# Linear attention, gated convolution and gMLP in one kernel: products of zeros on an idle TensorE, a corrected transfer model and new keys

## The chip, the cores and the metric

The kernel runs on one core of a Trainium2 chip. The metric is the device time of one launch in microseconds, the median of three runs. The core's engines are TensorE (PE, with its weight loads PEld), VectorE (DVE), ScalarE (ACT), GpSimd (POOL) and the SyncE queue (SP), which issues all transfers here.

## The reference

Three stages follow each other, with batch 8, sequence 576, and float32 inputs (weights arrive as 64-bit floats):

1. Attention with a feature map, for 8 heads of 64 columns: `phi(x) = [exp(p), exp(-p)]` with `p = x w_phi - max|x w_phi|`, 128 features. Then `kv = phi(k)^T v`, `z = sum phi(k)`, and the output is `phi(q) kv / (phi(q) z + 1e-6)`.
2. A gated convolution over 512 channels: `sigmoid(conv5(x)) * (x w_val)`, times `w_out`.
3. A gMLP: `h = relu(x w_in)` is cut into `u` and `v`, `v` is normalised over its 512 columns, mixed over the sequence by `w_spatial` (576 x 576) plus a bias, multiplied by `u`, and put through `moe2_w_out`.

## The kernel before, in words

**Tiling.** The heads go in pairs: 4 pairs in each of 8 batches, 32 pairs in all. A pair loads k, v and q with the head dimension on the partitions, projects them by `w_phi` (`project`), takes the maxima and exponentials (`kexp`, `qmax`, `qexp`), sums k's side against v (`kvacc`, `kvout`) and forms numerators and denominators (`num`) that `divide` brings together; the result is a tile of x. When the four pairs of a batch are done, `mlp` does the batch's convolution, the products with w_val, the second half (`vchunk`) and the first half (`uhalf`) of w_in, the spatial mixing (`spatial`) and the output (`outrows`). w_out and w_in are multiplied together once, at the start: `weights` forms 8 tiles `wg` and `wu` from four tiles of w_out and four of each half of w_in, so that stage 2's last product and stage 3's first are one. Large products are made three times with high and low parts (`three`); the attention's are in float32, each of which the trace shows as two matmul instructions.

**Weights.** `load_f64` brings a tile of 64-bit floats and rebuilds float32 from it by one ScalarE and four VectorE instructions. There are 20 such tiles and one small one for the convolution. All of this runs beside the attention of the first pairs. From pair 4 on (`WHOLE`) the last 64 rows of a pair are loaded on their own; from pair 5 on (`EARLY`) VectorE and ScalarE weigh the denominators ahead of TensorE.

**Memory.** Two arenas in SBUF (`fa` float32, `ra` rounded float32) and the 8 banks of PSUM (`pa`) are handed out by `Arena.take` and `Arena.give`, which for the first 150 us of the plan's time prefers places that have rested.

**The order.** Nothing is issued while the kernel is described: each operation goes into a `Plan` with the engines that could do it, a modelled duration and a key. `Plan.order` (L234) then simulates the five engines: at each event every free engine takes, among its ready operations, the one with the least key, if buffers are free, and if the key is no more than `WINDOW` over the oldest key not yet started. A key's unit is one batch. The constants at the top of the file (L33 to L43) place the keys of each kind of operation: `AK_...` and `AQ_...` for a pair's k and q sides (eighths of a batch), `W_...` for the weights, `M_...` for the mixing layers. `READY` is when each engine begins in the model, `Clock` a model of TensorE's clock, and `FA_HOLD` and `RA_HOLD` room that operations ahead of their time leave free. Transfers are modelled by one number, the time at which the last one has gone through. `Plan.emit` (L341) issues the operations in the order found; every engine then runs its own in that order, and waits for data by semaphores.

**Lines in the profile.** The helpers issue everything, so L396 is any ScalarE or VectorE instruction, L431 POOL, L441 a transfer, L452 the three-part products (`gemm`), L465 all other products (`products`).

The two lines that place the first pair's loads before (L758, L763):

```
plan.key = (t + sub) / 8 * A_RATE - A_LEAD
at(t, AK_LOAD)
```

Of the kernel before, what the change touches and what calls it, by code (L numbers as in the profile page):

```python
# [10 lines left out]
F32 = mybir.dt.float32  # L11
# [8 lines left out]
B, H, S, D = 8, 8, 576, 64  # L20
F = 128
# [4 lines left out]
REM = 512  # L26
# [1 line left out]
DZ = D + 1  # L28
HALF = S // 2
TSPLIT = ((0, 256), (256, 320))  # L30
COLS = 28896
FA_COLS = 18176
A_LEAD, A_RATE = 1.4787, 1.0  # L33
AK_LOAD, AK_PROJ, AK_ACC, AK_SUM, AK_TURN = -0.2236, -0.128, -0.555, 0.2361, 2.6811
AQ_LOAD, AQ_MAX, AQ_EXP, AQ_NUM, AQ_HEAD, A_DIV = -0.4346, -0.0325, 0.8218, 3.0598, -0.0974, 5.3953
W_VAL, W_CONV, W_OUT, W_G, W_U, W_SP, W_OUT2, W_STEP = -1.6328, -1.2064, -0.8762, -0.9691, -0.5711, 0.3701, 0.0606, 0.072
M_CONV, M_VAL, M_V, M_U, M_SP, M_OUT, M_ALL = -0.3169, -0.2374, -0.148, 0.1029, -0.3397, 0.1352, 57.899
LONG_W, LONG_A, LONG_M = False, False, True
WINDOW = 0.4378
FA_HOLD = 3522  # L40
RA_HOLD = 4422
PA_HOLD = 0
LATER = 0.3845  # L43

MODE = 0.2419

EARLY = 5

WHOLE = 4

REST, SOON = 6.0, 150.0
READY = {"PE": 0.0, "ACT": 2.0, "DVE": 0.9, "POOL": 1.1, "SP": 0.6}
SIGNAL = {"PE": 0.2, "ACT": 0.145, "DVE": 0.13, "POOL": 0.2, "SP": 0.06}


# [2 lines left out]
SWITCH = 0.1  # L58

HELD = 1.0  # L60


class View:
# [29 lines left out]
class Buf(View):  # L93


    def __init__(self, model, cols, arena=None):
        super().__init__(self)
        self.model, self.cols, self.arena = model, cols, arena
        self.place = None if arena else model
        self.at = None  # L100
        self.base, self.writes, self.reads = [], [], []
        self.left, self.until = 0, 0.0
        self.long = False

    def note(self, op, reads, writes):
        deps = list(self.base)
# [94 lines left out]
class Plan:  # L201
# [5 lines left out]
        self.ops = []  # L207
        self.key = 0.0

    def add(self, ways, reads, writes, modes=(FULL, FULL), dma=False):  # L210

        op = Op()
        op.ways = ways
        op.n = len(self.ops)
        op.key = self.key
        op.modes, op.dma = modes, dma
        op.users, op.ready, op.start, op.end, op.way = [], 0.0, None, None, None
        seen = {}
        for group, w in ((reads, 0), (writes, 1)):
            for v in group:  # L220
                r = seen.setdefault(id(v.buf), [v.buf, False, False])
                r[1 + w] = True
        op.bufs = [r[0] for r in seen.values()]
        deps = {}
        for b, r, w in seen.values():
            for d in b.note(op, r, w):
                if d is not op:
                    deps[id(d)] = d
        op.need = len(deps)
        for d in deps.values():  # L230
            d.users.append(op)
        self.ops.append(op)

    def order(self, window, hold):  # L234

        ops = self.ops
        waiting = {e: [] for e in self.ENGINES}
        free = dict(READY)
        events = [0.0] + list(free.values())
        heapq.heapify(events)  # L240
        transfers, clock, mode = 0.0, Clock(), FULL
        frees = []
        by_key = sorted((o for o in ops if "POOL" not in o.ways), key=lambda o: (o.key, o.n))
        oldest = 0
        done = []
# [30 lines left out]
        while len(done) < len(ops):  # L276
# [13 lines left out]
            while again:  # L290
# [4 lines left out]
                for e in self.ENGINES:  # L295
# [6 lines left out]
                    for op in ready:  # L302
# [4 lines left out]
                        if e == "PE":  # L307
# [3 lines left out]
                            op.end = now + clock.run(now, busy, until)  # L311
                            busy = op.end - now
                        if op.dma:
                            transfers = max(transfers, now + busy + 0.63) + until
                            op.end = transfers + 0.85
                        free[e] = now + busy
                        if e == "POOL" and busy > 1.0:
                            free["DVE"] = max(free["DVE"], now) + HELD
# [17 lines left out]
                        again = True  # L336
                        forced = False
                        break
        return done

    def emit(self, window, hold):  # L341
        for op in self.order(window, hold):
            for b in op.bufs:
                if b.place is None:
                    b.place = b.arena.model(b.at[0] * b.arena.step, b.cols)
            op.ways[op.way][2]()
# [3 lines left out]
def attn_moe_gmlp_kernel(  # L350
# [19 lines left out]
    ctx.enter_context(tc.manual_schedule())  # L370

    plan = Plan()
    fa_t = const.tile([128, FA_COLS], F32, name="fa")
    ra_t = const.tile([128, COLS - FA_COLS], F32R, name="ra")
    banks = [ps.tile([128, 512], F32, name=f"bank{i}") for i in range(8)]
    fa = Arena(lambda o, n: fa_t[:, o:o + n], FA_COLS, 16)
    ra = Arena(lambda o, n: ra_t[:, o:o + n], COLS - FA_COLS, 16)
    pa = Arena(lambda o, n: banks[o // 512][:, 0:n], 8 * 512, 512)

    def fixed(shape, dtype, name):  # L380

        t = const.tile([shape[0], -(-shape[1] // 32) * 32], dtype, name=name)
        return Buf(t[:, 0:shape[1]], shape[1])
# [5 lines left out]
    def views(*xs):  # L389
        return [x for x in xs if isinstance(x, View)]  # L390
# [41 lines left out]

        plan.add({"POOL": (t, t, run)}, ins, [dest])

    def dma(out, in_, engine="SP"):
        n = 1
        for d in (out.shape() if isinstance(out, View) else out.shape):
            n *= d

        def run():  # L440
            (nc.sync if engine == "SP" else nc.scalar).dma_start(out=real(out), in_=real(in_))  # L441

        rows = (out.shape() if isinstance(out, View) else out.shape)[0]
        plan.add({engine: (0.475 if rows == 128 else 0.65, 4 * n / 385e3, run)}, views(in_), views(out), dma=True)

    def gemm(acc, terms, first=True, last=True):
        n = len(terms)
# [34 lines left out]


    warm = fixed([128, 8], F32, "warm")
    wphi = fixed([128, F], F32, "wphi")
    k4 = [fixed([128, F], F32, f"k4_{i}") for i in range(3)]
    q4 = [fixed([128, F], F32, f"q4_{i}") for i in range(3)]
# [4 lines left out]
    wr1 = fixed([128, S], F32R, "wr1")  # L492
    convw = fixed([128, 5 * KD], F32, "convw")
    rden = [Buf(dr.tile([2, S], F32, name=f"rden{i}"), S) for i in range(4)]

    def wtiles(name, n, width):
        return [[fixed([128, width], F32R, f"{name}{i}_{k}") for k in range(n)] for i in range(2)]
# [28 lines left out]
    def weights():  # L526
        def at(x):
            plan.key = x

        at(-2.0)  # L530
        dma(wphi, w_phi.unsqueeze(0).to_broadcast([2, D, F]))

        def fill(x, value):
            pool(0.1 + cols_of(x) / 960, "memset", x, [], x, value)


        fill(ones, 1.0)
        fill(warm, 0.0)
# [62 lines left out]
    def load_k(P):  # L601
        b, hp = divmod(P, NP)
        kl, vl = k4[P % 3], v4[P % 3]
        n = S if P < WHOLE else REM
        k, v = fa.buf(n), fa.buf(4 * 2 * VW)
        dma(k, kT[b, hp, :, 0:n])
        dma(v.rearrange("p (c d) -> p c d", c=4), v1[b, 0:REM, hp].rearrange("(c p) d -> p c d", p=128))

        if P < WHOLE:
            vt = fa.buf(2 * VW)  # L610
            dma(vt, v1[b, REM:S, hp].unsqueeze(0).to_broadcast([2, 64, 2 * VW]))
        for hh in range(2):
            r, d, o = half(hh), vcols(hh), slice(DZ * hh, DZ * hh + DZ)
            if P < WHOLE:
                copy(kl[r, r], k[r, REM:S])
                copy(vl[r, o], vt[r, d])
            else:
                dma(kl[r, r], kT[b, hp, r, REM:S])
                dma(vl[r, o], v1[b, REM:S, hp, d])
        return k, v, kl, vl  # L620
# [134 lines left out]
    def attention():  # L755
        n = B * NP

        def at(t, sub=0.0):  # L758
            plan.key = (t + sub) / 8 * A_RATE - A_LEAD

        for P in range(n):
            t = 2 * P
            at(t, AK_LOAD)  # L763
            k, v, kl, vl = load_k(P)
            at(t, AQ_LOAD)
            q, ql = load_q(P)
            at(t, AK_PROJ)
            kas, qas = project(k, kl, q, ql)
            at(t, AK_ACC)
            kp = [kexp(a, 4) for a in kas[0:2]]  # L770
# [237 lines left out]
```

## Time and profile before

| | |
|---|---|
| median of 3 runs | 853.55 us (851.74 to 854.84) |
| profiled execution | 857.97 us, of which span 856.2 us |
| TensorE busy | 824.4 us, 96% of the span, 7800 instructions |
| VectorE busy | 653.9 us, 76% |
| ScalarE busy | 495.9 us, 58% |
| GpSimd busy | 148.7 us, 17% |
| mean granted TensorE clock | 0.992 |
| transfers | 62.29 MB, mean 73 GB/s |

Times in the trace count from the first instruction of the span. A line of the timeline has the start, the duration, the engine, the kernel's line, the operation, output and inputs with shape and type, how many like instructions are merged into it, and in brackets how long the engine stood before it and which engine's work ended that wait. A table by stretches has, for each stretch, its length, then the busy time and count of PE, PEld, DVE, ACT and POOL, TensorE's granted clock, the share of the transfer engines that is busy and the bytes moved. A busy TensorE is not TensorE at its peak: matmuls overlap, and the durations show the clock.

### The profile page before, as it was taken

Reading aid. Unit: us, or ns where it says so; the run is one execution under the profiler, and the core shown is the slowest. Engines: PE = TensorE matmul, PEld = TensorE weight load, DVE = VectorE, ACT = ScalarE, POOL = GpSimd, SP = SyncE. Lnnn points to the kernel's source line nnn. Section 1 sums busy time; section 2 is a strip of 40 time slices with the busy share of each in tenths; the row PEclk is TensorE's granted clock in tenths of the full one; section 3 lists DMA queues with packets and bytes.
Section 4 is the critical chain, followed back from the end, with each engine's and each line's share of the span. In section 5 each row is a group of like instructions: output and inputs, shape, how many; then the busy total and the mean of one; then the engine's idle time right before and its main releaser. Section 6 shows DMA issues by size and latency. Waiting matters only on the chain.

```text
span 856.2 us, 19859 instructions
## 1 busy us (share of the span) xinstructions
PE 824.4 (96%) x7800; PEld 676.9 (79%) x7800; DVE 653.9 (76%) x1531; ACT 495.9 (58%) x1069; POOL 148.7 (17%) x123
## 2 busy tenths in 40 slices
PE   4798999999999999999999999999999999999997
PEld 2544597787879787897878888797978888798896
DVE  5899999797798776985788866886788875965641
ACT  4876488766466655656466654756556573733321
POOL 3431042203011212103021221204022120100000
PEclk9999999999999999999999999999999999999999
DMA  7553414231322222131221232022221221001001
GB/s 233 170 185 100 144 45 137 51 84 60 79 54 51 77 74 68 30 86 46 69 71 37 81 97 67 30 63 69 81 59 47 60 82 51 17 21 52 13 8 62
DMA packets 64301, 62.29 MB, mean 73 GB/s; under 512 B 26574, under 2 KB 43598, under 8 KB 64208
## 3 DMA queue, kind: packets, MB, share of 16 engines
q1 hardware_dynamic: 64208, 61.02, 25.1%
q8 instruction: 61, 1.00, 0.5%
q14 instruction: 32, 0.26, 0.1%
HBM read 50.22 MB, written 9.58 MB: 70 GB/s over the span
## 4 chain that ended last, share of the span: by engine, by line
PE 72%; DMA 3%; DVE 3%; ACT 1%; issue 1%; SPq 0%; DVEq 0%; ACTq 0%
PE bank L452 54%; PE bank L465 18%; DVE fa L396 2%; DMA fa<-rden 2%; ACT fa L396 1%; DMA rden<-fa 1%; DMA out_dram<-fa 1%; DVE ra L396 0%; ACT ra L396 0%; DMA fa<-fa 0%; SPq L441 0%; DVE wr L396 0%; ACT wr L396 0%; DVEq L396 0%; ACTq L396 0%
## 5 line engine op out<-in xcount | busy, mean ns | idle before, releaser
L396 ACT ACTIVATE fa<-fa 128x512 f32<-128x512 f32 (+2 forms) x452 | 254.7, 628 | 49.0 <-DVE fa L396 36.2
L396 ACT ACTIVATE fa<-bank 128x512 f32<-128x512 f32 (+6 forms) x354 | 138.3, 440 | 187.4 <-PE bank L452 102.5
L431 POOL PARTITION_ALL_REDUCE fa<-fa x64 | 141.5, 2249 | 408.1 <-ACT fa L396 327.3
L465 PE MATMUL bank<-fa 128*64 128x65 f32 (+2 forms) x3216 | 173.7, 301 | 6.0 <-ACT fa L396 5.9
L465 PEld LDWEIGHTS bank<-fa 128*64 128x64 f32 (+2 forms) x3216 | 109.0, 131 | 80.0 <-issue 39.8
L396 ACT ACTIVATE ra<-fa 128x256 fp32r<-128x256 f32 (+4 forms) x192 | 87.8, 480 | 100.6 <-DVE fa L396 87.8
L396 DVE TENSOR_TENSOR fa<-fa 128x576 f32<-128x576 f32 (+2 forms) x240 | 112.3, 469 | 40.6 <-DMA fa<-rden 32.1
L396 DVE TENSOR_TENSOR ra<-fa,ra 128x256 fp32r<-128x256 f32 (+4 forms) x224 | 105.6, 495 | 17.8 <-ACT ra L396 14.7
L452 PE MATMUL bank<-wg,ra 128*128 128x512 f32 (+1 forms) x480 | 115.8, 394 | 0.0
L452 PE MATMUL bank<-ws,ra 128*128 128x256 f32 (+1 forms) x768 | 113.8, 298 | 0.4 <-DVE fa L396 0.4
L452 PEld LDWEIGHTS bank<-ra,wu 128*128 128x128 f32 x768 | 104.2, 189 | 5.8 <-issue 1.9
L452 PE MATMUL bank<-ra,wv 128*128 128x256 f32 (+1 forms) x768 | 107.0, 297 | 1.6 <-DVE fa L396 0.7
L452 PEld LDWEIGHTS bank<-ra,wv 128*128 128x128 f32 x768 | 103.7, 189 | 5.9 <-DVE fa L396 2.4
L452 PE MATMUL bank<-ra,wu 128*128 128x256 f32 (+1 forms) x768 | 107.1, 297 | 0.6 <-ACT fa L396 0.6
L452 PEld LDWEIGHTS bank<-ws,ra 128*128 128x128 f32 x768 | 106.5, 191 | 1.3 <-DVE fa L396 0.7
L396 DVE SCALAR_TENSOR_TENSOR fa<-fa,convw 128x576 f32<-128x576 f32 x128 | 105.9, 831 | 0.6
L452 PEld LDWEIGHTS bank<-wg,ra 128*128 128x128 f32 (+1 forms) x480 | 84.0, 177 | 26.0 <-issue 1.9
L452 PE MATMUL bank<-wo,ra 128*128 128x512 f32 x432 | 103.7, 395 | 0.0
L452 PEld LDWEIGHTS bank<-wo,ra 128*128 128x128 f32 x432 | 80.1, 188 | 21.4 <-issue 3.3
L396 DVE SCALAR_TENSOR_TENSOR fa<-fa 128x2 f32<-128x2 f32 (+4 forms) x192 | 89.6, 473 | 7.0 <-ACT fa L396 4.9
L396 DVE TENSOR_REDUCE fa<-bank 128x4 f32<-128x512 f32 (+1 forms) x96 | 50.9, 549 | 12.3 <-PE bank L465 11.2
L396 DVE BATCH_NORM_STATS2 fa<-fa 128x6 f32<-128x512 f32 (+1 forms) x40 | 27.6, 690 | 41.4 <-ACT fa L396 41.1
(62 smaller groups left out, 567.1 us busy)
## 6 DMA issues: line engine op xcount, KB each, us to landing
fa<-rden SPq DMA_DIRECT2D x64, 144.0 KB
fa<-in_v_dram SPq DMA_DIRECT2D x32, 264.0 KB
out_dram<-fa SPq DMA_DIRECT2D x32, 256.0 KB
fa<-in_qT_dram SPq DMA_DIRECT2D x28, 256.0 KB
fa<-in_kT_dram SPq DMA_DIRECT2D x28, 256.0 KB
fa<-in_w_in_dram SPq DMA_DIRECT2D x8, 512.0 KB
fa<-in_w_val_dram SPq DMA_DIRECT2D x4, 512.0 KB
fa<-in_w_outT_dram SPq DMA_DIRECT2D x4, 512.0 KB
```

The source lines that it names most:

```text
L396: return lambda: getattr(engine, method)(**{k: real(v) for k, v in kw.items()})
L431: getattr(nc.gpsimd, method)(*(real(a) for a in args), **{k: real(v) for k, v in kw.items()})
L452: nc.tensor.matmul(real(acc), lhsT=real(l), rhs=real(r), start=first and i == 0, stop=last and i == n - 1)
L465: nc.tensor.matmul(real(o), lhsT=real(l), rhs=real(r), start=first, stop=last)
```

## The change

Four things are done.

- *Zeros.* A tile of 128 x 128 zeros is set aside and cleared by POOL as its first work. In `order`, when TensorE is free, nothing is ready for it and less than 60 us of the plan's time have gone, one product of zeros by zeros is put there, into the free bank that has rested the longest; `emit` issues these between the other operations. Nothing reads their results.
- *Transfers.* The model now begins at 3.0 us, adds a time of landing by kind (into SBUF 1.35, out 0.3, within 0.85, instead of 0.85 for all), and lets a queue hold 1152 pieces at most: an issue that would exceed it keeps SP until an earlier one is through. This changes only the simulated times, and by them the order.
- *The first pair's key.* The loads and the projection of pair 0 have their keys shifted by `AK_FIRST`.
- *Keys.* All keys of the attention, the weights and the mixing layers, the window, the holds and the modelled starts are set anew. The arenas lose 128 columns to the zeros.

```diff
-COLS = 28896
+COLS = 28768
-AK_LOAD, AK_PROJ, AK_ACC, AK_SUM, AK_TURN = -0.2236, -0.128, -0.555, 0.2361, 2.6811
-AQ_LOAD, AQ_MAX, AQ_EXP, AQ_NUM, AQ_HEAD, A_DIV = -0.4346, -0.0325, 0.8218, 3.0598, -0.0974, 5.3953
-W_VAL, W_CONV, W_OUT, W_G, W_U, W_SP, W_OUT2, W_STEP = -1.6328, -1.2064, -0.8762, -0.9691, -0.5711, 0.3701, 0.0606, 0.072
-M_CONV, M_VAL, M_V, M_U, M_SP, M_OUT, M_ALL = -0.3169, -0.2374, -0.148, 0.1029, -0.3397, 0.1352, 57.899
+AK_FIRST, AK_LOAD, AK_PROJ, AK_ACC, AK_SUM, AK_TURN = -0.2622, -0.4275, -0.3266, -0.4232, 0.018, 2.3344
+AQ_LOAD, AQ_MAX, AQ_EXP, AQ_NUM, AQ_HEAD, A_DIV = -0.4244, -0.0448, 0.7936, 3.122, -0.3118, 5.3894
+W_VAL, W_CONV, W_OUT, W_G, W_U, W_SP, W_OUT2, W_STEP = -1.64, -1.1968, -1.028, -1.0159, -0.5941, 0.3247, 0.2234, 0.0713
+M_CONV, M_VAL, M_V, M_U, M_SP, M_OUT, M_ALL = -0.3158, -0.2205, -0.1374, 0.109, -0.3565, 0.0794, 57.899
-WINDOW = 0.4378
-FA_HOLD = 3522
-RA_HOLD = 4422
+WINDOW = 0.4982
+FA_HOLD = 3515
+RA_HOLD = 3926
-LATER = 0.3845
-MODE = 0.2419
+LATER = 0.3318
+MODE = 0.2164
-READY = {"PE": 0.0, "ACT": 2.0, "DVE": 0.9, "POOL": 1.1, "SP": 0.6}
+READY = {"PE": 1.0, "ACT": 2.0, "DVE": 0.9, "POOL": 0.6, "SP": 0.75}
+FLOW, LAND, RING = 3.0, {"in": 1.35, "out": 0.3, "own": 0.85}, 1152
+FILL = 60.0
...
     def order(self, window, hold):
+        self.fillers = {}
-        transfers, clock, mode = 0.0, Clock(), FULL
+        transfers, clock, mode = FLOW, Clock(), FULL
+        flying = []
...
                         if op.dma:
+                            kind, n = op.dma
+                            held = sum(f[1] for f in flying)
+                            for f in sorted(flying):
+                                if f[0] > now and held + n <= RING:
+                                    break
+                                held -= f[1]
+                                flying.remove(f)
+                                busy = max(busy, f[0] - now)
                             transfers = max(transfers, now + busy + 0.63) + until
-                            op.end = transfers + 0.85
+                            flying.append((transfers, n))
+                            op.end = transfers + LAND[kind]
...
+            if free["PE"] <= now < FILL and now >= READY["PE"]:
+                banks = self.banks
+                rested = [(banks.since[i], i) for g in banks.gaps for i in range(*g)]
+                if rested:
+                    at = min(rested)[1]
+                    mode = FULL
+                    free["PE"] = now + clock.run(now, 4 * F / 2400, 1.0)
+                    heapq.heappush(events, free["PE"])
+                    self.fillers.setdefault(len(done), []).append(at)
         return done
     def emit(self, window, hold):
-        for op in self.order(window, hold):
+        for n, op in enumerate(self.order(window, hold)):
+            for at in self.fillers.get(n, ()):
+                self.fill(at)
...
+    plan.fill = lambda at: nc.tensor.matmul(banks[at][:, 0:F], lhsT=zero.ap(), rhs=zero.ap(), start=True, stop=True)
+    plan.banks = pa
+    zero = fixed([128, F], F32, "zero")
...
+        at(-2.5)
+        fill(zero, 0.0)
         at(-2.0)
         dma(wphi, w_phi.unsqueeze(0).to_broadcast([2, D, F]))
...
-            at(t, AK_LOAD)
+            first = AK_FIRST if P == 0 else 0.0
+            at(t, AK_LOAD - first)
             k, v, kl, vl = load_k(P)
-            at(t, AQ_LOAD)
+            at(t, AQ_LOAD - first)
             q, ql = load_q(P)
-            at(t, AK_PROJ)
+            at(t, AK_PROJ - first)
```

## Rows read from the trace of the kernel before

**Rows 1.** The page: span, and busy time of each engine.

```profile
span 856.2 us, 19859 instructions
PE 824.4 (96%) x7800; PEld 676.9 (79%) x7800; DVE 653.9 (76%) x1531; ACT 495.9 (58%) x1069; POOL 148.7 (17%) x123
```

**Rows 2.** Table by stretches: busy PE, PEld, DVE, ACT, POOL; clock, DMA share, GB/s.

```profile
10.00:28.00 18.00, 12.93 (x120) 9.21 (x120) 15.54 (x25) 12.49 (x35) 9.63 (x6) 1.00 0.68 214
28.00:60.00 32.00, 28.64 (x414) 17.04 (x416) 27.17 (x58) 26.22 (x65) 10.14 (x7) 0.89 0.53 164
60.00:85.00 25.00, 21.46 (x190) 10.86 (x188) 24.22 (x46) 15.91 (x33) 5.02 (x4) 0.99 0.42 124
...
163.00:177.00 14.00, 10.94 (x121) 9.61 (x120) 12.12 (x25) 12.39 (x25) 0.10 (x1) 0.88 0.21 56
...
200.00:800.00 600.00, 598.35 (x5778) 506.50 (x5776) 458.38 (x1094) 344.50 (x739) 97.50 (x68) 1.00 0.22 59
800.00:857.00 57.00, 51.13 (x311) 46.05 (x310) 22.75 (x77) 14.91 (x29) 0.00 (x0) 0.99 0.09 31
```

**Rows 3.** Timeline of TensorE, early projections, sums and weights' products, and later ones.

```profile
10.24 0.77 PE L465 MATMUL bank<-wphi,k 128*128 128x128 f32 x2 [10.24 <-ACT k L396]
...
16.91 0.77 PE L465 MATMUL bank<-wphi,k 128*128 128x128 f32 x2 [1.76 <-ACT k L396]
...
21.75 2.73 PE L465 MATMUL bank<-fa 128*64 128x65 f32 x64
...
28.44 0.46 PE L465 MATMUL bank<-wphi,k 128*128 128x128 f32 x2 [3.52 <-POOL fa L431]
...
31.94 5.83 PE L465 MATMUL bank<-fa 128*32 128x288 f32 x112
...
42.33 3.12 PE L465 MATMUL bank<-fa 128*32 128x288 f32 x48
...
50.66 4.69 PE L465 MATMUL bank<-fa 128*32 128x288 f32 x48 [1.09 <-ACT fa L396]
...
60.86 19.40 PE L465 MATMUL bank<-fa 128*128 128x512 f32 x144
...
84.19 18.74 PE L465 MATMUL bank<-fa 128*32 128x288 f32 x80 [3.48 <-ACT fa L396]
102.76 0.39 PE L465 MATMUL bank<-wphi,k 128*128 128x128 f32 x2
102.98 0.39 PE L465 MATMUL bank<-q,wphi 128*128 128x128 f32 x2
...
105.25 9.47 PE L452 MATMUL bank<-ra,wv 128*128 128x256 f32 x72
...
117.05 2.09 PE L465 MATMUL bank<-fa 128*64 128x65 f32 x64
```

**Rows 4.** Timeline of VectorE, two of the instructions that rebuild a weights' tile.

```profile
9.06 0.42 DVE L396 TENSOR_SCALAR fa<-fa 128x512 f32<-128x512 f32 x1
...
9.39 0.69 DVE L396 SCALAR_TENSOR_TENSOR fa<-fa 128x512 uint32<-128x512 uint32 x1
```

**Rows 5.** Timeline around the first spatial products: a late load, and TensorE's waits.

```profile
163.05 0.68 ACT L396 ACTIVATE wr<-fa 128x576 fp32r<-128x576 f32 x1 [5.02 <-DMA fa<-in_w_spT_dram]
...
170.67 0.39 PE L452 MATMUL bank<-wr,ra 128*128 128x256 f32 x1 [0.48 <-DMA ra<-ra]
...
172.63 0.39 PE L452 MATMUL bank<-wr,s 128*128 128x256 f32 x1 [1.57 <-DVE wr L396]
```

**Rows 6.** The chain of waits, the same piece two batches apart.

```profile
303.48 29.65 PE bank L452 x168
...
498.85 29.56 PE bank L452 x168
```

**Rows 7.** The first pair's v on SP, and bytes moved in 0 to 20 us.

```profile
3.41 1.10 SPq L441 DMA_DIRECT2D fa<-in_v_dram  x2
...
GB/s 0 0 0 0 0 129 127 356 386 419 401 382 404 344 372 345 288 280 335 362 370 370 307 302 349 382 352 217 124 66 59 49 50 71 241 309 331 282 271 217
```

More of the change, by code (lines that the diff above doesn't have):

```diff
@@ L102, in __init__ @@
         self.left, self.until = 0, 0.0
-        self.long = False
+        self.long, self.dram = False, False
     def note(self, op, reads, writes):
@@ L208, in __init__, with add @@
         self.key = 0.0
-    def add(self, ways, reads, writes, modes=(FULL, FULL), dma=False):
+    def add(self, ways, reads, writes, modes=(FULL, FULL), dma=None):
         op = Op()
@@ L433, in pool, with dma @@
         plan.add({"POOL": (t, t, run)}, ins, [dest])
-    def dma(out, in_, engine="SP"):
+    def dma(out, in_, engine="SP", pieces=None):
         n = 1
@@ L443, in dma @@
         rows = (out.shape() if isinstance(out, View) else out.shape)[0]
-        plan.add({engine: (0.475 if rows == 128 else 0.65, 4 * n / 385e3, run)}, views(in_), views(out), dma=True)
+        kind = "own" if views(in_) and views(out) else "in" if views(out) else "out"
+        if kind == "own" and (in_.buf.dram or out.buf.dram):
+            kind = "in" if in_.buf.dram else "out"
+        plan.add({engine: (0.475 if rows == 128 else 0.65, 4 * n / 385e3, run)}, views(in_), views(out),
+                 dma=(kind, pieces or rows))
     def gemm(acc, terms, first=True, last=True):
@@ L494, in attn_moe_gmlp_kernel @@
     rden = [Buf(dr.tile([2, S], F32, name=f"rden{i}"), S) for i in range(4)]
+    for r in rden:
+        r.dram = True
     def wtiles(name, n, width):
@@ L528, in at, with fill @@
             plan.key = x
+        def fill(x, value):
+            pool(0.1 + cols_of(x) / 960, "memset", x, [], x, value)
+        at(-2.5)
+        fill(zero, 0.0)
         at(-2.0)
         dma(wphi, w_phi.unsqueeze(0).to_broadcast([2, D, F]))
-        def fill(x, value):
-            pool(0.1 + cols_of(x) / 960, "memset", x, [], x, value)
         fill(ones, 1.0)
@@ L606, in load_k @@
         dma(k, kT[b, hp, :, 0:n])
-        dma(v.rearrange("p (c d) -> p c d", c=4), v1[b, 0:REM, hp].rearrange("(c p) d -> p c d", p=128))
+        dma(v.rearrange("p (c d) -> p c d", c=4), v1[b, 0:REM, hp].rearrange("(c p) d -> p c d", p=128), pieces=512)
         if P < WHOLE:
```

## The prediction

> **What bounds the kernel now.** I read the shares of the page first, then the busy time by stretches, then TensorE's timeline of the first 60 us, the chain of waits, and last the timelines around the two places where TensorE still stands. TensorE is busy for 96% of the span [rows 1], so this is a TensorE kernel: its time is the products at full clock, plus what it stands, plus what it loses at the half clock. The table by stretches says where the standing lies [rows 2]: 5.1 us in 10 to 28, 3.4 in 28 to 60, 3.5 in 60 to 85, 3.1 in 163 to 177, 1.65 in the whole of 200 to 800, 5.9 in the last 57 (the last output's way out), and 10.2 before the first product [rows 3]. So there is almost nothing left to win behind 200 us; some 25 us lie ahead of 177 us.
>
> The half clock must be read from durations. [...] Where the column falls to 0.89 (28 to 60) and 0.88 (163 to 177), TensorE had stood just before: 3.52 us at 28.44, 1.09 at 50.66 [rows 2, 3].
>
> The second thing to see is VectorE: 15.5 of 18 us busy in 10 to 28, 27.2 of 32 in 28 to 60, 24.2 of 25 in 60 to 85 [rows 2]. Early on TensorE is fed by VectorE (and ScalarE, 26.2 of 32), which turns the weights' double words into floats between the pairs' work. VectorE's own idle time from 10 to 85 us, 75 minus 66.9, is 8.1 us; no order of the same work can bring the products of that stretch forward by more unless it chooses other work to do first.
>
> **The change part by part.** I sum against the profiled execution, 857.97 us (span 856.2 and 1.8 around it), which is 4.4 us over the median of the runs, 853.55; the difference is carried over to the median.
>
> *A. Zeros keep the clock up until 60 us of the plan's time.* What the half clock costs, from [rows 3]: projections 4.91 - 2.49 = 2.42 and 4.84 - 2.49 = 2.35; the 64 products at 21.75, 2.73 - 2.09 = 0.64; the projection at 28.44, 3.50 - 2.49 = 1.01; the 112 at 31.94, 5.83 - (3.12 + 2.09) = 0.62; the 48 at 50.66, 4.69 - 3.12 = 1.57. Together 8.6 us. Not all of it is on the path. The first three (5.4 us) end ahead of the 3.52 us that TensorE stands before 28.44: had they been shorter, it would have stood longer, since the second pair's operands and ScalarE's exponentials set the next starts. The last three (3.2 us) lie in stretches where TensorE then runs on with little idle. I take 3.2; the ends are 0 and 8.6.
>
> *B. The weights' tiles come sooner against the fourth pair.* From the keys: the four tiles of w_out and the four of w_in's second half all go ahead of the loads of pair 3 now (their keys end at -0.802, the pair's begin at -0.782); before, five did. One tile costs VectorE 2 x 0.42 + 2 x 0.69 = 2.2 us [rows 4], so the products of the weights (before at 60.86, and the 19.4 us of TensorE work that this row shows need nothing but the tiles [rows 3]) can begin up to 6.7 us sooner, and fill the 3.4 us of idle in 28 to 60; pair 3 and what hangs on it come later by as much VectorE time. TensorE's idle in 28 to 85 is 6.9 us [rows 2], the upper end. The lower end is -6.7, pair 3 late and nothing in its place. I take +2.5, about a third of the idle, since VectorE's own idle (8.1 us over 75) leaves room for no more than that when the whole of 60 to 85 is full.
>
> *C. The stall at 163 to 177.* TensorE waits there for the last tiles of the spatial weights: the load that ScalarE waited 5.02 us for, then two products 0.48 and 1.57 us late [rows 5]. Idle 3.06 and 14 x 0.12 = 1.7 of half clock: 4.7 us [rows 2]. W_SP goes 0.045 earlier and the spatial product's own key 0.017; a batch is 97.7 us (from 303.48 to 498.85 two batches [rows 6]), so the tiles gain 4.4 - 1.6 = 2.8 us on the product. That is more than the waits of 2.05, though the vector work moved ahead of them is full as well. I take +2.0; ends 0 and 4.7.
>
> *D. The first pair's own key.* It puts the first load of q behind k and v (keys -1.4994 and -1.4990; before q came first at -1.5330). v's two transfers are 264 and 66 KB; at some 380 GB/s of the early slices [rows 7] that is 0.9 us. They take SP 1.10 us to issue [rows 7]. The first projection needs q and k and not v, so it may start up to 1.1 us later. Much of this is covered by the 1.76 us that TensorE stands right behind the pair. I take -0.5; ends -1.1 and +0.5.
>
> *E. The zeros themselves.* Each is one product of 128x128 in float32, two instructions, 0.22 us apart at full clock (102.76 to 102.98 [rows 3]), twice that at half. TensorE's idle before 60 us, 18.4 [rows 2], holds 40 to 85 of them. SP and POOL give nothing but one memset. A zero product that stands in the queue when a true one is ready delays it by half its length on average, and there are seven gaps: 7 x 0.11 to 7 x 0.22 = 0.8 to 1.5 us. The zeros also wait for the last reader of their bank. Behind a late one everything on TensorE stands, and ScalarE and VectorE for its results; a reader of a bank takes 0.4 to 0.7 us, so seven of those cost 5 at worst. I take -0.5, since the gaps end where ScalarE is late and not TensorE.
> [...]
>
> *F. The corrected transfers, the 128 columns that the zeros take from the second arena, the holds and the other keys.* The transfer model changes no instruction; it changes the order that comes out. Behind 200 us it can win no more than the 1.65 us of idle there [rows 2], and it can lose one stall such as C's, 4.7. I take -0.5, near to the row of what there is to win.
>
> Sum: 3.2 + 2.5 + 2.0 - 0.5 - 0.5 - 0.5 = 6.2 us. The profiled execution would be 851.8, the median 847.4.
>
> **The rivals.** *R1, VectorE hides it.* The zeros warm the clock and TensorE only stands longer: early it is fed by VectorE and ScalarE, whose instructions don't shrink. For it: 24.2 of 25 us in 60 to 85, and the 3.48 us wait for ScalarE at 84.19 [rows 2, 3], which a TensorE that is 3 us ahead at 55 merely meets sooner. Against it: VectorE has 8.1 us of idle before that, some of which is waiting for TensorE. A and B are then worth 0, C 2.0, D to F -1.5: 0.5 us, median 853.
>
> *R2, slower: batch 0 starves.* Three tiles more go ahead of pair 3, 6.7 us of VectorE [rows 4]. The first batch's mixing layers can't begin before pair 3 is divided; if the weights' products and pairs 4 and 5 don't last until then, TensorE stands ahead of 105.25. It decides from the point where the fourth pair is later than the weights' products are sooner. Price: 6.7 late, less 3.2 of A, with D to F against it by 1.5 and C not reached in time: 5.0 slower, 858.5. Against it: from 84.19 on TensorE ran 18.7 us without a break before the next projection [rows 3], so it had work in stock.
>
> *R3, the zeros don't raise the clock* (it doesn't do what it says). If it takes data that toggle, A goes and E stays: 3.0 better than before, 850.5. No row of before shows a product of zeros. [...]
>
> *R4, a new stall late in the run.* Each key changes, and one stall of C's size behind 200 us takes away 4.7 and the clock after it; with R1's start this is 4 slower, 857.5.
>
> **How the numbers follow.** My forecast has 0.58, R1 0.22, R2 0.11, R3 0.04, R4 0.05. A difference of 0.3% (2.6 us) is about what can be told from none here. Faster: 0.58, R3's most (0.03) and a little of R1's upper side: 0.62. Same: 0.21. Slower: R2 and R4 with R1's lower edge: 0.17. The low end takes A at 8 and B at 5 with the rest as it is, 13.5 us less, 840; the high end reaches into R2 and R4, 857. About 0.08 lies on either side. The likeliest case's own range is 843 to 851.
>
> **What would show it.** A: two-instruction products of zeros from about 1 us on, the first projection near 2.5 us long and no half-clock durations until 60 us; what TensorE stands before 60 without the zeros then says whether true work moved. B: the weights' products start ahead of 60.86, and TensorE's idle time at 80 to 84 is shorter. C: the last spatial tile lands some 4 us sooner against its first product, and 163 to 177 is full. D: the first true product at 10 to 11.4 us. E: TensorE's gaps end by ScalarE or VectorE and not behind a zero product that waits for its bank. F: idle in 200 to 800 within 3 us of 1.65. The forecast is wrong if the weights' products start no sooner and TensorE's work done by 85 us is the same (R1), or if there is a gap ahead of the first batch's mixing (R2).

## The result and the profile after

The changed kernel takes 860.12 us (median of 9 runs, 856.78 to 864.88) against 853.55 us for the kernel before (9 runs, 851.5 to 855.61): a ratio of 1.0061, 95% interval 1.004 to 1.0083. It is slower, where a gain to 847.4 us was predicted. The profiled execution took 862.86 us, with a span of 861.1 and a mean granted clock of 0.991; the nine runs go with that clock, from 856.78 us at 0.998 to 864.88 at 0.990.

The page, span and busy time by engine, as in [rows 1]:

```profile
span 861.1 us, 20282 instructions
PE 843.3 (98%) x8002; PEld 699.9 (81%) x8002; DVE 663.0 (77%) x1519; ACT 498.6 (58%) x1081; POOL 153.7 (18%) x124
```

TensorE is busier (98% for 96%) and the kernel is longer. It issues 202 instructions more, which are the 101 products of zeros. Busy time now holds work that nobody needs, so the idle column can no longer be read as loss, or its absence as gain.

The table by stretches (columns as in [rows 2]; the last two rows split the first 10 us of the second):

```profile
0.00:10.00 10.00, 9.01 (x58) 9.01 (x59) 1.94 (x5) 3.14 (x5) 3.81 (x27) 1.00 0.71 229
10.00:28.00 18.00, 14.84 (x149) 11.95 (x149) 11.77 (x21) 9.90 (x29) 7.79 (x5) 0.81 0.81 264
28.00:60.00 32.00, 31.78 (x456) 24.17 (x451) 28.68 (x55) 26.80 (x67) 12.36 (x7) 1.00 0.43 127
80.00:90.00 10.00, 9.90 (x196) 6.08 (x190) 8.81 (x16) 8.41 (x19) 4.22 (x4) 1.00 0.65 187
163.00:177.00 14.00, 10.98 (x66) 9.73 (x66) 8.97 (x18) 10.46 (x21) 1.68 (x1) 0.76 0.11 31
200.00:800.00 600.00, 595.38 (x5762) 502.57 (x5762) 465.35 (x1079) 345.27 (x742) 100.47 (x68) 1.00 0.22 60
10.00:15.00 5.00, 1.84 (x13) 1.46 (x13) 3.19 (x6) 2.21 (x6) 0.00 (x0) 0.82 0.85 291
15.00:20.00 5.00, 5.00 (x28) 3.50 (x27) 4.12 (x10) 2.29 (x8) 0.73 (x1) 0.50 0.53 141
```

28 to 60 runs at a granted clock of 1.00 (0.89 before), but 10 to 15 is nearly empty, and right behind that, in 15 to 20, the granted clock is 0.50. 163 to 177 stands as long as before (3.02 us for 3.06) at a lower clock (0.76 for 0.88 [rows 2]). In 200 to 800, 4.6 us are idle instead of 1.65.

TensorE's timeline (start, us, operation, count of instructions, and in brackets what it stood for before):

```profile
0.99 9.50 PE L402 MATMUL bank<-zero 128*128 128x128 f32 x60 [0.99 <-POOL zero L462]
...
10.32 0.39 PE L500 MATMUL bank<-wphi,k 128*128 128x128 f32 x2
...
13.87 0.77 PE L500 MATMUL bank<-q,wphi 128*128 128x128 f32 x2 [3.16 <-ACT q L427]
...
22.09 0.39 PE L500 MATMUL bank<-wphi,k 128*128 128x128 f32 x2
...
31.84 0.46 PE L500 MATMUL bank<-wphi,k 128*128 128x128 f32 x2
...
51.63 0.49 PE L500 MATMUL bank<-wphi,k 128*128 128x128 f32 x2
...
64.62 15.92 PE L500 MATMUL bank<-fa 128*128 128x512 f32 x96
...
111.42 9.48 PE L487 MATMUL bank<-ra,wv 128*128 128x256 f32 x72
...
167.80 3.57 PE L487 MATMUL bank<-ra,wu 128*128 128x320 f32 x12 [3.02 <-ACT fa L427]
...
504.63 3.11 PE L487 MATMUL bank<-ra,wv 128*128 128x256 f32 x24 [0.63 <-ACT fa L427]
...
509.79 4.86 PE L487 MATMUL bank<-ra,wv 128*128 128x256 f32 x36 [2.05 <-DVE fa L427]
```

The zeros do what they are for: the first product of k, at 10.32, takes 0.39 us and not 0.77 [rows 3]. Then TensorE stands 3.16 us for q, and the product that follows takes 0.77 again. The second, third and fourth projections start at 22.09, 31.84 and 51.63; the second and third stood at 16.91 and 28.44 [rows 3].

ScalarE and the SP queue in the same execution, the first 14 us and around 160:

```profile
2.94 1.50 SPq L472 DMA_DIRECT2D fa<-in_v_dram  x2
...
4.49 2.11 SPq L472 DMA_DIRECT2D fa<-in_qT_dram  x1
...
12.13 0.53 ACT L427 ACTIVATE v<-fa 64x65 f32<-64x65 f32 x2 [2.30 <-DMA fa<-in_v_dram]
...
13.22 0.51 ACT L427 ACTIVATE q<-fa 64x64 f32<-64x64 f32 x2
...
155.16 0.58 SPq L472 DMA_DIRECT2D fa<-in_w_spT_dram  x1
...
164.32 1.39 ACT L427 ACTIVATE wr<-fa 128x576 fp32r<-128x576 f32 x2 [4.77 <-DMA fa<-in_w_spT_dram]
```

Both places have one pattern: ScalarE waits for a transfer that lands late (v's last rows; the last rows of the spatial weights), and what it would do next, q's copies at 13.22, stands behind that wait. The bytes moved in 150 to 170 us, in slices of 0.5 us (DMA: busy tenths of the 16 engines), show the second of them:

```profile
DMA  0131673310010208698995112111111100000010
GB/s 1 24 41 70 207 230 104 72 27 11 0 34 15 28 14 124 190 308 226 344 311 148 62 51 83 51 46 49 52 41 48 41 4 0 0 0 0 0 9 0
```

From 161 to 166 bytes trickle at 41 to 83 GB/s, with a busy share of one or two tenths. The load of the spatial rows was issued at 155.16 and its reader starts at 164.32, so what trickles after that is no longer this load; k, v and q of a later pair were issued behind it, from 156.68 to 157.64, and whose bytes they are the view does not show.

Last, the chain of waits, three stretches of 160 products (the 112 of a batch's spatial mixing and 48 with `wu` ahead of them or behind), here and then in the kernel before:

```profile
261.71 22.12 PE bank L487 x160
...
360.36 22.09 PE bank L487 x160
...
560.77 22.13 PE bank L487 x160
```

```profile
260.74 22.13 PE bank L452 x160
...
359.41 22.02 PE bank L452 x160
...
554.68 22.09 PE bank L452 x160
```

At 261 and at 360 us the changed kernel is 1.0 us late; at 560 it is 6.1 us late; from there to the end of the span it wins 1.2 back (300.3 us for 301.5; the four other kernels with the old order below take 300.0 to 300.4, so the 1.2 is a matter of this execution of the kernel before). That makes the 4.9 us between the two spans (861.1 and 856.2), beside 5.2 by the ratio (0.0061 of 853.55) and 6.6 by the medians; the profiled execution of the kernel before, 857.97 us, lies above all nine of its runs here. So in these two executions the early part, where nearly the whole forecast lay, is about even, and most of the loss arises between 360 and 555.

### The profile page after: what moved, and what is told of

It reads as the page before. It is cut to its first block, busy times and chain, and to the rows that moved or that the text cites. A ratio compares the mean times of both kernels' runs of the same rounds, so it can differ in the third digit from the quotient of the medians.

```text
span 861.1 us, 20282 instructions
## 1 busy us (share of the span) xinstructions
PE 843.3 (98%) x8002; PEld 699.9 (81%) x8002; DVE 663.0 (77%) x1519; ACT 498.6 (58%) x1081; POOL 153.7 (18%) x124
## 4 chain that ended last, share of the span: by engine, by line
PE 85%; DMA 5%; DVE 5%; ACT 3%; issue 1%; SPq 1%; ACTq 0%; DVEq 0%
PE bank L487 60%; PE bank L500 24%; DVE fa L427 4%; ACT fa L427 3%; DMA fa<-in_w_spT_dram 1%; DMA fa<-in_v_dram 1%; DMA fa<-rden 1%; SPq L472 1%; DMA rden<-fa 1%; DMA fa<-in_w_in_dram 1%; PE bank L402 0%; DVE ra L427 0%; DMA q<-in_qT_dram 0%; DMA fa<-fa 0%; DVE wg L427 0%
## 5 line engine op out<-in xcount | busy, mean ns | idle before, releaser
L427 ACT ACTIVATE fa<-fa 128x576 f32<-128x576 f32 (+3 forms) x453 | 256.9, 630 | 67.0 <-DVE fa L427 49.2
L462 POOL PARTITION_ALL_REDUCE fa<-fa x64 | 147.1, 2336 | 498.4 <-ACT fa L427 328.0
L427 ACT ACTIVATE fa<-bank 128x288 f32<-128x288 f32 (+6 forms) x358 | 140.3, 437 | 152.1 <-PE bank L487 81.9
L500 PE MATMUL bank<-fa 128*64 128x65 f32 (+2 forms) x3216 | 168.5, 294 | 0.7 <-DVE fa L427 0.6
L500 PEld LDWEIGHTS bank<-fa 128*64 128x64 f32 (+2 forms) x3216 | 107.1, 129 | 67.0 <-issue 30.3
L427 ACT ACTIVATE ra<-fa 128x256 fp32r<-128x256 f32 (+6 forms) x198 | 88.4, 466 | 121.6 <-DVE fa L427 106.2
L427 DVE TENSOR_TENSOR fa<-fa 128x2 f32<-128x2 f32 (+2 forms) x240 | 108.8, 458 | 34.4 <-DMA fa<-rden 24.8
L427 DVE SCALAR_TENSOR_TENSOR fa<-fa,convw 128x576 f32<-128x576 f32 x128 | 112.1, 876 | 2.1 <-ACT fa L427 1.3
L487 PE MATMUL bank<-ra,wu 128*128 128x256 f32 (+1 forms) x768 | 109.8, 299 | 3.7 <-ACT fa L427 3.7
L427 DVE TENSOR_SCALAR fa<-fa 128x2 f32<-128x2 f32 (+7 forms) x184 | 47.4, 272 | 21.0 <-ACT fa L427 10.6
```

The costliest lines, as they stand in the source:

```text
L427: return lambda: getattr(engine, method)(**{k: real(v) for k, v in kw.items()})
L462: getattr(nc.gpsimd, method)(*(real(a) for a in args), **{k: real(v) for k, v in kw.items()})
L487: nc.tensor.matmul(real(acc), lhsT=real(l), rhs=real(r), start=first and i == 0, stop=last and i == n - 1)
L500: nc.tensor.matmul(real(o), lhsT=real(l), rhs=real(r), start=first, stop=last)
```

## The experiments

My theory on the result was that the zeros were worth nothing because the projections waited for v and q, and that the loss came from transfers that land late; the rivals were that the zeros themselves did harm, that q behind v did it, and that the order made with the new keys was worse later on. All twelve are compared with the kernel before, on the same chip, medians 854.13 to 854.22 us. "Halves" stands for one edit: three loads that put the same rows on both halves of the partitions (w_phi, v's last rows, the last rows of the spatial weights) are issued as two transfers of 64 partitions instead of one whose outermost dimension is 2. The order and its model are left as they are. Differences in us below are of the medians, where nothing else is said.

| kernel | median us | ratio (95%) |
|---|---|---|
| changed, no zeros | 859.79 | 1.0068 (1.0042 to 1.0094) |
| changed, halves | 852.01 | 0.9979 (0.9962 to 0.9996) |
| changed, q ahead of v | 860.09 | 1.0077 (1.005 to 1.0103) |
| before, zeros | 852.14 | 0.9982 (0.9964 to 1.0) |
| before, halves | 845.34 | 0.9895 (0.9874 to 0.9917) |
| before, halves and zeros | 847.96 | 0.9924 (0.9904 to 0.9944) |
| changed, spatial rows halved | 856.43 | 1.003 (1.0012 to 1.0047) |
| changed, w_phi and v halved | 857.78 | 1.0042 (1.0026 to 1.0058) |
| changed, old keys | 878.51 | 1.0277 (1.0246 to 1.0308) |
| before, new keys | 869.33 | 1.0157 (1.0132 to 1.0182) |
| before, halves and few zeros | 845.67 | 0.9883 (0.9856 to 0.991) |
| changed, halves, no zeros | 856.97 | 1.0021 (0.9999 to 1.0043) |

**The changed order without its zeros** (e1_no_zeros).

```
-    plan.fill = lambda at: nc.tensor.matmul(banks[at][:, 0:F], ...)
+    plan.fill = lambda at: None
```

> The changed kernel with the same order of all true work, and no products of zeros. If the zeros do what they are for and the loss lies in the order, this is slower than the changed kernel (860.1): the first two projections fall back to 4.9 us each and the mean clock to about 0.985, end 861 to 864. If the zeros stand in the way of true products (in the changed kernel the second pair's operands are there at 20.9 us and its first product waits for zeros until 22.1), it is faster, 857 to 859. If VectorE and ScalarE hide both, 859.5 to 861.

859.79 us, no difference from 860.12 that these runs could tell. Taken together the zeros neither help nor harm in this order. The first product of q starts at 13.32, only 0.55 us sooner than with them, so the operands set it and not the zeros:

```profile
13.32 0.76 PE L500 MATMUL bank<-q,wphi 128*128 128x128 f32 x2 [3.28 <-ACT q L427]
```

**The old order with zeros in its gaps** (e4_before_zeros).

```
+ZEROS = {224: 28, 273: 18, 243: 9, 322: 17, 341: 9, 349: 4, 446: 14}
...
+                        if op.n in ZEROS:
...
+                            self.fillers[op.n] = [min(rested)[1]] * ZEROS[op.n] if rested else []
```

> The kernel before in its own order, with products of zeros put into TensorE's measured gaps alone (28 ahead of the first product, 18, 9, 17, 9, 4 and 14 ahead of six others until 84 us). If the half clock is on the path, 3.2 us as the prediction took it: 849 to 851. If VectorE and ScalarE hide it: 852.5 to 854.5, with the early projections at 2.5 us all the same. If the zeros delay true work: 855 or more.

852.14 us, 0.9982: 1.5 us by the ratio, 2.1 by the medians, and the interval just touches no change. The first batch's product of the mixing starts at 102.75 instead of 105.25 [rows 3]:

```profile
102.75 9.49 PE L465 MATMUL bank<-ra,wv 128*128 128x256 f32 x72
```

So term A exists in the old order, 2.5 us at that place where 3.2 was taken. In the changed order the same product starts at 111.42 with zeros and at 111.29 without.

**q ahead of v for the first pair** (e3_q_first).

```
+for move, ahead in ((222, 216), (223, 219), (224, 219)):
+    queue.remove(where[move])
+    queue.insert(queue.index(where[ahead]), where[move])
```

(222 is q's transfer, 216 v's; 223 and 224 are q's copies on ScalarE, 219 v's first.)

> The changed kernel, same order but for the first pair: q's transfer ahead of v's, and q's two copies on ScalarE ahead of v's. If the first pair is late because ScalarE takes its instructions in order and v's copies wait for v until 12.1 us, q's first product comes at 10.3 to 10.6 instead of 13.9, the standing of 3.2 us and the half clock in 15 to 20 go, and the pairs behind are 2 to 4 us sooner. Whether this reaches the end: 855 to 858 if the early loss is the loss; 859 to 861 if it is made up by 120 us (the first batch's second product was only 1.1 us later than in the kernel before) and the rest is lost in 160 to 177 and 400 to 560.

860.09 us. The first product of q does come at 10.48, 3.4 us sooner, and then the second pair stands as long for v:

```profile
10.48 0.46 PE L508 MATMUL bank<-q,wphi 128*128 128x128 f32 x2 [0.22 <-ACT q L435]
...
19.11 0.76 PE L508 MATMUL bank<-wphi,k 128*128 128x128 f32 x2 [3.12 <-ACT v L435]
```

The first pair's key moved the wait and made none of the loss that shows at the end.

**The late loads, all three halved** (e2_halves in the changed kernel, e5_before_halves in the old one).

```
     def run():
-        (nc.sync if engine == "SP" else nc.scalar).dma_start(out=real(out), in_=real(in_))
...
+            else:
+                for h in range(2):
+                    q.dma_start(out=real(out[64 * h:64 * h + 64]), in_=twice)
...
-        dma(t, w_spT[REM:S].unsqueeze(0).to_broadcast([2, 64, S]))
+        dma(t, w_spT[REM:S].unsqueeze(0).to_broadcast([2, 64, S]), twice=w_spT[REM:S])
```

> The changed kernel, same order; the loads that copy 64 rows onto both halves of the partitions (w_phi, the last rows of v, the last rows of the spatial weights) go as two transfers of 64 partitions instead of one with a leading dimension of 2. The trace shows 46 to 55 GB/s while the spatial rows load, about 2 of 16 engines' share. If such a load runs on two engines, the spatial rows land 4 us or more sooner, the 3.0 us wait at 164 to 168 and the half clock behind it go, v of the first pair lands 1 to 3 us sooner: 853 to 857. If they are late for another reason (bytes ahead in the queue), the landing stays at 9 us and the end at 859 to 861.

> The kernel before in its own order, with the loads onto both halves of the partitions as two transfers of 64 partitions each. The stall at 163 to 177 (4.7 us) waits for the same spatial rows, so it should go here too, 849 to 851. If the kernel before was faster than the changed one because its order hid these loads, nothing is won: 853 to 855. If the two-engine loads are a cost of both orders and the new keys are otherwise no better, this is below the changed kernel with the same loads (852.0).

852.01 us, 8.1 less than the changed kernel; and 845.34, 8.8 less than the kernel before. The bytes moved in 150 to 170 us of the changed order with halves, which is 3.9 us ahead there (it issues the spatial rows at 151.28 and not at 155.16):

```profile
DMA  0100169647999700100000000001900010005762
GB/s 11 27 1 22 27 120 249 231 86 184 297 322 377 298 25 0 33 0 0 0 0 0 0 0 0 4 5 25 217 21 0 0 9 0 16 0 88 226 230 75
```

The trickle is gone; by 157.5 nearly all is moved. ScalarE's copies, here of v's last rows and of the spatial rows, the issue of the latter, and the stretch 163 to 177, in the same execution:

```profile
9.56 0.54 ACT L427 ACTIVATE v<-fa 64x65 f32<-64x65 f32 x2 [1.09 <-DMA fa<-in_v_dram]
...
151.28 1.18 SPq L477 DMA_DIRECT2D fa<-in_w_spT_dram  x2
...
155.54 1.42 ACT L427 ACTIVATE wr<-fa 128x576 fp32r<-128x576 f32 x2
...
163.00:177.00 14.00, 14.00 (x115) 13.12 (x114) 13.90 (x29) 11.17 (x24) 0.00 (x0) 1.00 0.17 40
```

v's copy is 2.6 us sooner than 12.13. The spatial copy is 8.8 sooner than 164.32 and without a wait: 3.9 of that is the earlier issue, 4.9 the time from issue to reader, 4.3 us for 9.2. The stretch is full (14.00 of 14) at a granted clock of 1.00. In the old order the spatial copy starts at 154.20 instead of 163.05 [rows 5], 5.4 us behind its issue (148.79) and not 10.5 (152.53):

```profile
154.20 0.68 ACT L396 ACTIVATE wr<-fa 128x576 fp32r<-128x576 f32 x1
...
163.00:177.00 14.00, 13.19 (x104) 12.81 (x101) 13.77 (x28) 9.18 (x17) 0.10 (x1) 1.00 0.34 86
```

Both orders carried this cost, so it isn't what made the change slower.

**Only one kind halved** (e7_halves_spatial, e8_halves_v; the same edit on the spatial rows alone, or on w_phi and v alone).

> The changed kernel, same order, only the spatial weights' last rows loaded in two halves. If the stall at 164 to 168 and the clock behind it are one part of the 8 us that both loads gave: 854 to 857, with the start as in the changed kernel (first batch's second product at 111 us). If all of it came from the start: 859 to 861.

> The changed kernel, same order, only w_phi and v's last rows loaded in two halves. The first projection is complete at 13.7, the second begins at 16.7, the first batch's second product at 107.5 instead of 111.4; the stall at 164 stays. 855 to 857 if the start counts to the end; 859 to 861 if the stall behind takes the gain back.

856.43 and 857.78 us: 3.7 and 2.3 less than 860.12, together 6.0 of the 8.1. Four intervals of about 1.5 us each stand behind the 2.1 that are left, so that the two don't simply add is not shown. With the spatial rows halved alone, issued at 155.65 and thus as late as in the changed kernel, their copy starts 5.1 us later (160.79) without a wait, and 163 to 177 is at a granted clock of 1.00 with 0.67 us idle. With v halved alone ScalarE still waits 4.68 us for the spatial rows, and TensorE stands 3.24 us ahead of 163.

**Halves with zeros, with fewer, and with none** (e6_before_both, e11_few_zeros in the old order; e12_halves_no_zeros in the changed one).

From e6 to e11:

```
-ZEROS = {224: 28, 273: 18, 243: 9, 322: 17, 341: 9, 349: 4, 446: 14}
+ZEROS = {224: 26, 273: 10, 322: 14, 341: 6, 390: 12}
```

> The kernel before in its own order, with zeros in the measured gaps and the loads in two halves. If the two effects add (zeros 2.1 us, loads 3 to 5): 846 to 849. If the faster loads empty the gaps that the zeros were counted for, so that zeros then delay true products: 850 to 852.

> The kernel before in its own order, loads in two halves, and zeros only where that kernel with halved loads still stood: 26 ahead of the first product, then 10, 14, 6 and 12. If the half clock costs what it cost in the order before (2.1 us) and the zeros end before the true products are ready: 842.5 to 844.5. If the zeros are hidden: 845 to 846. If they are in the way as with the 126 of the run with both: 847 or more.

> The changed kernel, same order, loads in two halves, no zeros. If the zeros stand in the way once the loads are early (as in the order before, 2.6 us): 849 to 851. If they are worth nothing either way, as with the late loads: 851 to 853. If they keep the clock up to some use: 853 to 856.

In the old order the full counts (99 products, not the 126 of the expectation) cost 2.6 us (847.96 for 845.34; the two intervals just overlap), fewer cost nothing (845.67). In the changed order, with halves, the zeros are worth 5.0 (852.01 with, 856.97 without), 3.6 by the two ratios. The old order with halves, without zeros and then with the full counts:

```profile
14.77 0.46 PE L470 MATMUL bank<-wphi,k 128*128 128x128 f32 x2 [0.30 <-ACT k L396]
...
24.19 0.46 PE L470 MATMUL bank<-wphi,k 128*128 128x128 f32 x2 [3.79 <-POOL fa L431]
```

```profile
12.20 4.29 PE L384 MATMUL bank<-zero 128*128 128x128 f32 x36
...
16.32 0.39 PE L483 MATMUL bank<-wphi,k 128*128 128x128 f32 x2
...
23.48 4.06 PE L384 MATMUL bank<-zero 128*128 128x128 f32 x34
...
27.38 0.39 PE L483 MATMUL bank<-wphi,k 128*128 128x128 f32 x2
```

The zeros were counted for gaps that the halves had shortened: the third projection started at 24.19 and now starts behind 34 zero instructions at 27.38. And the changed order with halves but no zeros:

```profile
28.00:60.00 32.00, 24.66 (x356) 15.57 (x356) 28.32 (x56) 25.81 (x65) 10.98 (x5) 0.88 0.47 138
```

TensorE stands for 7.3 of these 32 us at a clock of 0.88. With the late loads and no zeros it is much the same there (7.95 us, 0.89 in e1), where zeros are worth nothing, so this row alone does not tell where they pay. The difference has come by the first batch's first product with `wg`: 116.87 with zeros and 121.33 without; with the late loads 120.73 and 120.60. That late operands set the starts in the latter case is likely and not shown.

**Keys and model apart** (e9_old_keys: the changed code with all keys, window and holds of before; e10_new_keys: the code of before with all of the new ones, no zeros).

```
-AK_FIRST, AK_LOAD, AK_PROJ, AK_ACC, AK_SUM, AK_TURN = -0.2622, -0.4275, -0.3266, -0.4232, 0.018, 2.3344
...
+AK_FIRST = 0.0
+AK_LOAD, AK_PROJ, AK_ACC, AK_SUM, AK_TURN = -0.2236, -0.128, -0.555, 0.2361, 2.6811
...
```

> The changed kernel with all keys, window and holds of the kernel before and no key of its own for the first pair; zeros and the corrected transfer model stay. If the new keys are what makes it slower (v ahead of q, the loss of 2.5 to 6 us in 360 to 560): 850 to 855, that part of the run as in the kernel before (195 us from the product at 359 to the one at 555). If the transfer model orders it worse whatever the keys: 857 to 863.

> The kernel before with the new keys, window and holds and the first pair's own key; no zeros, old transfer model. If the new keys are what makes it slower: 857 to 863, v ahead of q at the start and ScalarE waiting for it. If they are only slow together with the new transfer model: 851 to 856.

878.51 and 869.33 us, 24 and 15 slower than before. Neither half of the change can be had alone, which suggests that keys fit the model of transfers with which they were set. In 400 to 600 TensorE is idle for 0.07 us in the first and 0.64 in the second, against 4.4 in the changed kernel: neither half alone brings the loss in the middle. Much of their own loss lies ahead of it, such as 3.9 us idle in 85 to 120 in the first, and in the second 9.6 idle in 28 to 60 at a clock of 0.79. Which key costs the time in the middle when both are together, they do not say.

## Why the prediction was wrong

The steps that failed are F, C and B; A was right about the clock (1.00 for 0.89 in 28 to 60) and wrong about this order.

**F, the rest of the order: -0.5 taken, about -4.8 came.** I bounded it by what there was to win behind 200 us (1.65 [rows 2]) and by one stall of C's size, and then took the value at the end that wins. From the start of the 160 products near 359 us to that near 555, the kernels with the old order take 195.27 (before), 194.76, 195.09, 194.58 and 194.13 us (zeros, halves, both, few zeros): mean 194.8. Those with the new order take 200.41 (changed), 197.82, 198.72, 201.36, 199.36, 201.06 and 198.04 (no zeros, halves, q first, spatial, v, halves without zeros): mean 199.5. Every one of seven lies above every one of five, whatever was done to zeros or loads. Here most of the loss was made. TensorE's idle in 400 to 600 is 2.1 to 4.4 us in the seven and 0 to 1.1 in the five, 3.1 of the 4.8 in the mean; the rest is not accounted for. In the changed kernel it is 4.4 us, with the two waits at 504.63 and 509.79 shown above; VectorE, two microseconds ahead of the first, waits for a pair's divisors:

```profile
502.62 0.76 DVE L427 TENSOR_TENSOR fa<-fa 128x576 f32<-128x576 f32 x1 [4.70 <-DMA fa<-rden]
```

All seven have this wait, 3.2 to 4.7 us at 494 to 503. But the wait alone can't be the cause: in the five VectorE waits for divisors even longer in 400 to 600 (7.2 to 12.3 us in all, against 4.6 to 6.5), and TensorE hardly stands. What stands behind it in the new order and not in the old is not tested; which of the keys, the window, the holds and the 128 columns brings it stays open, as does why the piece in the other kernels varies by 3.5 us. It is R4's mechanism, near R4's size, to which I gave 0.05.

**C, the stall at 163 to 177: a gain of 2.0 taken, none came.** In this execution idle 3.02 and 14 x 0.24 = 3.4 of half clock make 6.4, against 4.7. The half clock is not there in every execution: in e1 and e3, with the same late load, TensorE stands 1.18 and 2.77 us at this place and the twelve products with `wu` behind take 2.05 and 2.03 us, not 3.57. The tiles did gain on their product, as C said: the first product with `wr` comes 12.0 us behind the start of ScalarE's copy (164.32) where it was 7.6 (163.05 to 170.67 [rows 5]), and the spatial products no longer wait:

```profile
176.30 0.28 PE L487 MATMUL bank<-wr,ra 128*128 128x256 f32 x1
```

What I had wrong is who waits. TensorE now stands ahead of products with `wu` (167.80), for work that ScalarE does behind that copy. The load takes 9.2 us from issue to its reader; [rows 5] showed ScalarE waiting 5.02 us for it, and I took it for a matter of order. e2, e5 and e7 show that it is the shape of the transfer: as two transfers of 64 partitions it had its reader 4.3 us (e2) and 5.4 us (e5) behind the issue, where the single one took 9.2 and 10.5.

**B, the weights' products: +2.5 taken, they came later.** 64.62 instead of 60.86 [rows 3]. The early pairs are 3.4 to 6.3 us later (31.84 for 28.44 [rows 3]; the fourth 51.63 for 45.38, which in the kernel before is this line):

```profile
45.38 0.49 PE L465 MATMUL bank<-wphi,k 128*128 128x128 f32 x2
```

One sign came as said: the idle at 80 to 84 went (9.90 busy of 10 in 80 to 90). The first batch's mixing product at 111.42 has one stretch of sums (2.46 us) ahead of it that stood behind before. By 261 us the two orders are 1.0 apart. R2's place was not where most was lost. With halved loads, where both orders are rid of the late ones, the new one gains nothing at the start either: its piece near 350 us begins at 352.46 with zeros and 356.42 without, the old order's at 349.64 without and 349.65 with few.

**A, the clock: +3.2 taken, 0 came in this order.** 28 to 60 ran at 1.00, but by the first batch's mixing product nothing was gained (111.42 with zeros, 111.29 without, e1). R1 described this: the next start is set by ScalarE and VectorE. I had measured R1 against VectorE's idle; at the first pair it was ScalarE, standing in order behind v's late copies.

**D, the first pair's key: at most 1.1 late taken, 3.1 came.** The first product of k starts as before (10.32 for 10.24 [rows 3]), but q's comes at 13.87, where in the kernel before it follows at once:

```profile
10.80 0.63 PE L465 MATMUL bank<-q,wphi 128*128 128x128 f32 x2
```

I summed bytes and issue time. The copies of q wait on ScalarE behind those of v, and v's last rows land late for the reason of C (their copy starts at 12.13, with halves at 9.56, e2). It cost the end nothing (e3).

**E, zeros in the way: -0.5 taken, 0 measured** (e1), and 2.6 where their counts no longer fit the gaps (e6). Single products were delayed all the same: the second pair's copies are done at 20.91, and its first product comes behind zeros at 22.09. There were 101 products, above the 40 to 85 estimated.

The forecast summed six terms as if each gap were the engine's own. The late loads, at the start and at 163, were a cost of both orders, and the part of the change that I called small and costed by the idle time that was left was the one that decided. The fastest version is the old order with halved loads: 845.34 us; few zeros beside them change nothing (845.67).

## What to carry to other kernels

Where an engine waits for a transfer, look at the rate at which it moves before moving its issue: a load at 52 GB/s, an eighth of the 419 that the early slices reach [rows 7], may be slow by its shape, as here, where the new keys left ScalarE's wait for it at 4.77 us (5.02 before) and two halves took the wait away. Filling idle time with dummy work was worth between a loss of 2.6 us and a gain of 5.0 here, by the order and the loads beside it, so its counts must be fitted to the gaps again after every other change; that it pays where the clock and not the operand sets the next start fits these runs. Where an order is made anew by a planner, cost the stretches that are full as the ones with most to lose, and give one stall there a real chance.

## What the runs showed of the hardware

**The spatial rows, loaded with an outermost dimension of 2, moved at about 50 GB/s.** In the changed kernel 46 to 83 GB/s moved in the last 3 us ahead of the reader of these 288 KB, with one or two tenths of the DMA engines busy; as two transfers of 64 partitions, issued at 151.28 (e2), the same bytes were in ahead of 155.54, and the slices between reach 297 GB/s. This is the kernel before in the last 3 us ahead of the reader (163.05 [rows 5]); its last issue before that is at 156.67 (the last two columns are DMA share and GB/s):

```profile
160.00:163.00 3.00, 3.00 (x22) 3.00 (x21) 0.00 (x0) 0.00 (x0) 1.80 (x1) 1.00 0.13 52
```

A share of 0.13 is what two busy engines of 16 would give (0.125), at some 26 GB/s each. So the two engines in the expectations are an estimate from this share; which engines were busy the view does not show.

**Products of zeros held the granted clock up.** After 60 zero instructions the first product of k took 0.39 us, where 0.77 stood in [rows 3] and in the same order without zeros (e1); 28 to 60 ran at a granted clock of 1.00 with them and 0.89 without (e1). R3 is out.

**The clock fell behind some waits, and the price came after them.** 3.16 us of standing at 10.7 was followed by a granted clock of 0.50 in 15 to 20. The granted clock of a stretch can also stand at 1.00 where products take twice as long: in 10 to 28 of the kernel before it is 1.00 [rows 2], yet a pair's projection took 4.91 us there (10.24 to 15.15) and 2.49 us later (102.76 to 105.25) [rows 3]. So the half clock is told here by durations. Twelve products with `wu` took 3.57 us behind a wait of 3.02 in the changed kernel (167.80), and the same twelve 2.03 us behind a wait of 2.77 in e3; in [rows 3] 48 products took 4.69 us behind a wait of 1.09 (50.66) and 3.12 without one (42.33). So the length of the wait alone does not tell the price.
